# Holding two output chunks of each batch over into the next batch's up phase (landmark attention into a gated product, one core)

## The chip, the core and the metric

The kernel runs on one NeuronCore of a Trainium2 chip. The metric is the device time in microseconds; where several executions are named, it is their median.

## What is computed

There are 8 batches of 8 heads, 576 tokens and head size 64. Queries and keys are averaged over 18 neighbouring tokens into 32 landmarks. Three softmax matrices, an iterated inverse of the 32 x 32 one, and v make the attention; its result, 512 wide, goes through two projections that are multiplied with each other, and two further weights.

```python
A  = sm(q, k_lm);  Bm = sm(q_lm, k_lm);  C = sm(q_lm, k)
Z  = Bm.T / (norm1(Bm) * norminf(Bm) + 1e-06)
for _ in range(6):
    Z = 2 * Z - Z @ Bm @ Z
x = (A @ Z @ C @ v)                 # (batch, tokens, heads*64) -> 4608 x 512
out = (((x @ w1) * (x @ w2)) @ w3) @ w_out      # 4608 x 512, float32
```

## The kernel before, in words

A prologue loads the weights and multiplies `w3 @ w_out` once into `w34` (function `fold`), beside the attention of batch 0. The eight batches then follow. Two things run beside each other in each of them.

The first is the product of batch `b`. `up(st, j, w)` makes one *unit*: four matmuls of 288 columns (line 433) into a PSUM tile `big`. For `w == 0` (called u here) ScalarE copies it to `a_sb` (line 437); for `w == 1` (called v) VectorE multiplies it with `a_sb` into the product tile `ab` (line 439). Sixteen units, j from 0 to 7, fill the 1024 rows of `ab` for the 576 tokens of a batch. `ab` holds two batches, so an even batch has four whole chunks of 128 tokens and an odd one five. `down` makes one *half* of a chunk's output: four matmuls of 512 columns (line 451) into a PSUM bank; after the second half ScalarE scales it into `o_sb` (line 460), and SP's queue writes it out (line 467).

The second is the attention of batch `b + 1`, a generator, advanced one stage at a time by `steps(at)`:

- stage 1: scores of four heads, `big`, exponent on ScalarE (lines 211, 215); the first partial sums on POOL (222 to 227)
- stage 2: the 32 x 32 landmark matrix `psB` (238), its exponent `ebm` (242), then row sums, reciprocal, product and transpose on VectorE (245 to 251)
- stage 3: scores of the other four heads; the norm on VectorE (261 to 268)
- stage 4: `psR` (300) into the one bank of `acc`, read by four VectorE operations (306, 308); `scores_a` (285); two `cv` products with v (317), the first into `small`, the second into `acc`
- stages 5 to 10: the six inverse steps, it0 to it5, each 16 small matmuls into a `big` tile (376), then `tz` and `sz` on VectorE (381, 383), which the next step needs; it0 to it2 add a reciprocal (346), it3 `rhi` and `rmix`, it5 the first `normalise` (361, 364)
- stage 11: `psZ` in `small` (398) and the second `normalise`
- stages 12 and 13: `g`, the weights of the next batch's units (419), moved out by ScalarE and VectorE (423, 425)

The PSUM tiles are three of `big` (two banks each) and one each of `small` and `acc`. The kernel is built under a manual schedule: each engine runs what it is given in the order of the program text, so the calls in the last loop are the order of the work.

For batch `b + 2` three more things are woven in: `turn_all` issues its transposing DMAs on SP (line 106) at the start of the batch; `load_v_piece` puts a small ScalarE copy and a DMA on SP (84, 85); `sums` and `landmarks` run on POOL (176 to 181, 196), with a ScalarE copy `far` in each `landmarks` (195). `sums` also issues the loads of batch `b + 3` from POOL.

In the loop before, the up phase takes stages 1 to 4 of the attention: after units u1, u2, u4 and u6. Stage 5 (it0) follows the last unit. The down phase then takes all chunks of the batch (8 halves in an even batch, 10 in an odd one), with one further stage after each half: it1 to it5, psZ, g, g. The chunks alternate between `acc` and `big`.

Of the kernel before, what the change touches and what calls it, by code (L numbers as in the profile page):

```python
# [13 lines left out]
B = 8  # L14
H = 8
S = 576
# [9 lines left out]
NP = 96  # L26
# [5 lines left out]
def kernel(  # L32
# [20 lines left out]
    def big():  # L53
        return psp.tile([128, 2, 512], FP32, name="big", bufs=3)

    def small():
        return psp.tile([128, 512], FP32, name="small", bufs=1)
# [22 lines left out]
    def load_v_piece(st, b, i, done):  # L80
        if i == 0:
            st["vt"] = pin.tile([128, H, 384], FP32, name="vt")
        hs = slice(2 * i, 2 * i + 2)
        nc.scalar.copy(out=st["vt"][0:NP, 2 * i, 0:1], in_=done)
        nc.sync.dma_start(out=st["vt"][0:NP, hs],
                          in_=v[b, hs].rearrange("h (p r) d -> p h (r d)", p=NP))

    def qk_pieces(st, b):
        st["qkn"] = pin.tile([128, 2, H, 384], FP16, name="qkn")
        for t, src in ((0, q), (1, k)):  # L90
            for i in range(2):
                hs = slice(4 * i, 4 * i + 4)
                nc.gpsimd.dma_start(out=st["qkn"][0:NP, t, hs, :],
                                    in_=src[b, hs].rearrange("h (p r) d -> p h (r d)", p=NP))
                yield
# [29 lines left out]
    ident = consts.tile([128, 128], FP32, name="ident")  # L125
# [45 lines left out]
    def sums(st, t, pieces=iter(())):  # L171
        st["o"] = st.get("o", {})
        o = st["o"][t] = pz.tile([128, H, 32], FP32, name="o%d" % t, bufs=1)
        x = st["qkT"][:, t]
        tr = pat.tile([128, H, NP], FP32, name="tr", bufs=1)
        nc.gpsimd.tensor_tensor(out=tr, in0=x[:, :, 0, :], in1=x[:, :, 1, :], op=ALU.add)  # L176
        nc.gpsimd.tensor_tensor(out=tr, in0=tr, in1=x[:, :, 2, :], op=ALU.add)  # L177
        next(pieces, None)
        t3 = tr.rearrange("p h (l g) -> p h l g", g=3)
        nc.gpsimd.tensor_tensor(out=o, in0=t3[:, :, :, 0], in1=t3[:, :, :, 1], op=ALU.add)  # L180
        nc.gpsimd.tensor_tensor(out=o, in0=o, in1=t3[:, :, :, 2], op=ALU.add)  # L181
        next(pieces, None)

    def landmarks(st, t, parity):
        o = st["o"][t]
        own, other = slice(64 * parity, 64 * parity + 64), slice(64 - 64 * parity, 128 - 64 * parity)
        if parity == 0:
            st["far"] = pz.tile([128, H, 32], FP32, name="far%d" % t, bufs=1)
            if t:
                st["lm"] = pat.tile([128, H, 32], FP16, name="lm")  # L190
            else:
                st["qbd"] = qbds.pop(0)
                qbds.append(st["qbd"])
        far = st["far"]
        nc.scalar.copy(out=far[own], in_=o[other])  # L195
        nc.gpsimd.tensor_tensor(out=st["lm"][own] if t else st["qbd"][own, :, parity, :],  # L196
                                in0=o[own], in1=far[own], op=ALU.add)


    def attention(st, bank=None):  # L200
        bank = bank or small
# [30 lines left out]
        yield  # L232

        lm = st["lm"]
        psB = bank()
        for qd in range(2):
            for h in range(4):
                nc.tensor.matmul(psB[32 * h:32 * h + 32, 32 * qd:32 * qd + 32],
# [129 lines left out]
        for it in range(6):  # L368
# [3 lines left out]
            for h in range(4):  # L372
                for qd in range(2):
                    sl = slice(32 * h, 32 * h + 32)
                    t = h ^ qd
# [34 lines left out]
        g = st["g"] = pat.tile([128, 2, 2, DF], FP16, name="gt")  # L410
# [18 lines left out]
    def up(st, j, w):  # L429
        p = big()  # L430
        for qd in range(2):
            for c in range(2):
                nc.tensor.matmul(p[:, c, 0:HS], st["g"][:, qd, w, 128 * j:128 * j + 128],  # L433
                                 st["ahat"][qd][:, c, :], start=(qd == 0), stop=(qd == 1))
        if w == 0:
            st["a_sb"] = po.tile([128, 2, HS], FP16, name="a_sb", bufs=2)
            nc.scalar.copy(out=st["a_sb"], in_=p[:, :, 0:HS])  # L437
        else:
            nc.vector.tensor_tensor(  # L439
                out=st["ab"][:, j, st["t0"]:st["t0"] + S].rearrange("p (c s) -> p c s", c=2),  # L440
                in0=st["a_sb"], in1=p[:, :, 0:HS], op=ALU.mult)
# [4 lines left out]
    def down(ab, b0, t0, half, hold, bank):  # L446
        if half == 0:
            hold["ps"] = bank()
        pso = hold["ps"]
        for j in range(4 * half, 4 * half + 4):  # L450
            nc.tensor.matmul(pso[:, :], ab[:, j, t0:t0 + 128], w34[:, j, :],  # L451
                             start=(j == 0), stop=(j == 7))
        if half == 1:
            o_sb = po.tile([128, DM], FP32, name="o_sb")
            final = b0 == B - 2 and t0 == 2 * S - 128
            if final:
                nc.vector.tensor_scalar(out=o_sb[:, 256:DM], in0=pso[:, 256:DM],
                                        scalar1=1.0 / (X64 * X64), scalar2=None, op0=ALU.mult)
            c = slice(0, 256 if final else DM)
            nc.scalar.activation(out=o_sb[:, c], in_=pso[:, c], func=AXF.Copy,  # L460
                                 scale=1.0 / (X64 * X64))
            o = 0
            while o < 128:
                gi, p0 = divmod((t0 + o) % S, NP)
                n = min(128 - o, NP - p0)
                eng = nc.scalar if final and o else nc.sync
                eng.dma_start(out=rows[b0 + (t0 + o) // S, 2 * (gi % 3) + gi // 3, p0:p0 + n, :],
                              in_=o_sb[o:o + n, :])
                o += n
# [48 lines left out]
    sts = [dict() for _ in range(B)]  # L518
# [4 lines left out]
    def turn_all(b):  # L523
        for t in (0, 1):
            for h0 in (0, 4):
                transposes(sts[b], t, range(h0, h0 + 4))

    def steps(g, n=1):
        for _ in range(n):
            next(g, None)  # L530
# [3 lines left out]
    with tc.tile_pool(name="pf", bufs=2) as pf:  # L534
# [67 lines left out]
        turn_all(1)  # L602
        steps(fd, 5)
        at = attention(sts[0])
        for n, m in enumerate((2, 2, 3, 3, 2, 1, 1, 1, 1, 2, 2, 3, 3)):
            steps(at)
            if n == 0:
                load_w3(7)
            elif n == 3:
                pieces = qk_pieces(sts[2], 2)  # L610
# [13 lines left out]
        steps(fd, 64)  # L624
    pab = ctx.enter_context(tc.tile_pool(name="pab", bufs=2))
    at = attention(sts[1], acc)


    for b in range(B):
        st = sts[b]  # L630
        if b % 2 == 0:
            ab = pab.tile([128, 8, 2 * S], FP16, name="ab")
        st["ab"], st["t0"] = ab, S * (b % 2)
        if b + 2 < B:
            turn_all(b + 2)
        chunks = range(0, 512, 128) if b % 2 == 0 else range(512, 2 * S, 128)
        for j in range(8):
            up(st, j, 0)
            if b + 1 < B and j == 0:
                landmarks(sts[b + 1], 1, 1)  # L640
            steps(at, (0, 1, 1, 0, 1, 0, 1, 0)[j])
            if b + 2 < B and j > 5:
                load_v_piece(sts[b + 2], b + 2, j - 6, ident[0:NP, 0:1])
            up(st, j, 1)
            if b + 2 < B and j == 5:
                pieces = qk_pieces(sts[b + 3], b + 3) if b + 3 < B else iter(())
                sums(sts[b + 2], 0, pieces=pieces)
                sums(sts[b + 2], 1, pieces=pieces)
        steps(at, 1)
        hold = {}  # L650
        nd = 2 * len(chunks)
        for n in range(nd):
            bank = (lambda: big()[:, 0, :]) if n // 2 % 2 else acc
            down(ab, b - b % 2, chunks[n // 2], n % 2, hold, bank)
            if b + 2 < B and n in (1, 3):
                load_v_piece(sts[b + 2], b + 2, 2 + n // 2, ident[0:NP, 0:1])
            steps(at)
            if b + 2 < B and n in (3, 4, 6):
                landmarks(sts[b + 2], n // 6, (n == 4) + 0)
        steps(at, 30)  # L660
        if b + 2 < B:
            at = attention(sts[b + 2], acc)


# [28 lines left out]
```

## Time and profile before

| what | value |
|---|---|
| median of 7 runs | 281.69 us (279.96 to 286.26) |
| the profiled execution | 280.25 us |
| its span, first to last instruction | 278.5 us |
| TensorE matmul | busy 265.2 us |
| VectorE | busy 164.5 us |
| ScalarE | busy 137.0 us |
| POOL | busy 162.5 us |
| matmuls of the units, line 433 | 512, mean length 286 ns |
| VectorE product, line 439 | 64, mean 749 ns |
| ScalarE copy, line 437 | 64, mean 639 ns |
| matmuls of the output halves, line 451 | 288, mean length 381 ns |

In the profile PE is TensorE's matmuls, PEld its weight loads, DVE VectorE, ACT ScalarE, POOL GpSimd and SP SyncE. The length given for a matmul overlaps with the next one, so distances between starts tell more than lengths. A line of the timeline has start and length in microseconds, engine, source line, tiles written and read, the count of merged instructions, and in brackets the idle time of the engine before it and what ended it.

### The profile page before, as it was taken

The page shows a single profiled execution, that of the slowest core. Times are in us where ns is not written, and L with a number is a line of the kernel's source. Part 1 is how long each engine was busy: PE and PEld are TensorE (multiplying, and loading weights), DVE is VectorE, ACT ScalarE, POOL GpSimd, SP SyncE. Part 2 cuts the span into 40 slices and gives each one's busy share as a digit, 9 for nine tenths or more (in the row PEclk, how much of TensorE's full clock was granted, in tenths as well). Part 3 has the DMA queues.
Part 4 walks back from the last instruction along what each step waited for, and adds up shares of the span by engine and source line. Part 5 has one row for each costly group of instructions (what it writes and reads, how often), then busy time and mean ns, then how long its engine had stood idle before and what let it go on. Part 6 is the DMA issues. An engine that isn't in the chain of part 4 may idle for free.

```text
span 278.5 us, 9481 instructions
## 1 busy us (share of the span) xinstructions
PE 265.2 (95%) x3964; PEld 148.3 (53%) x3964; DVE 164.5 (59%) x439; ACT 137.0 (49%) x259; POOL 162.5 (58%) x210
## 2 busy tenths in 40 slices
PE   7999999999999999999999989999999999999992
PEld 3456555444674476446645744575467346744741
DVE  7744135652476677657765865577668655766710
ACT  2644453144663663466348623762485356615531
POOL 1626862496479759935995699269956944400000
PEclk9999999999999999999999999999999999999998
DMA  6999999999918995999699769895997442014024
GB/s 207 321 239 253 229 271 159 168 277 139 145 44 147 262 170 133 195 213 162 139 209 217 153 133 213 198 162 113 243 225 102 129 153 72 2 47 109 3 75 113
DMA packets 61978, 45.57 MB, mean 164 GB/s; under 512 B 35568, under 2 KB 54000, under 8 KB 61936
## 3 DMA queue, kind: packets, MB, share of 16 engines
q1 hardware_dynamic: 47280, 31.93, 49.6%
q0 software_dynamic: 13824, 11.54, 28.8%
q10 hardware_dynamic: 832, 1.51, 1.5%
q8 instruction: 31, 0.51, 0.8%
q14 instruction: 11, 0.09, 0.1%
HBM read 38.80 MB, written 9.44 MB: 173 GB/s over the span
## 4 chain that ended last, share of the span: by engine, by line
PE 74%; DVE 12%; ACT 8%; issue 3%; DMA 1%; POOL 1%; ACTq 0%; DVEq 0%
PE acc L451 13%; PE big L433 13%; PE acc L497 12%; PE big L451 11%; DVE ab L439 7%; PE big L376 6%; PE big L419 4%; PE small L317 2%; PE big L361 2%; PE small L497 2%; ACT a_sb L437 2%; PE big L484 2%; PE acc L317 2%; ACT gt L423 2%; PE big L211 2%
## 5 line engine op out<-in xcount | busy, mean ns | idle before, releaser
L433 PE MATMUL big<-ahat,gt 128*128 128x288 f16 x512 | 72.8, 286 | 3.3 <-ACT a_sb L437 1.7
L439 DVE TENSOR_TENSOR ab<-a_sb,big 128x576 f16<-128x576 f16 x64 | 47.4, 749 | 24.6 <-ACT a_sb L437 16.1
L433 PEld LDWEIGHTS <-gt 128*128 128x128 f16 x512 | 48.4, 98 | 22.3 <-issue 9.8
L437 ACT CAST a_sb<-big 128x576 f16<-128x576 f32 x64 | 40.9, 639 | 32.2 <-PE big L433 32.1
L497 PE MATMUL acc<-wsp,w3t 128*128 128x512 f16 x168 | 41.1, 380 | 2.0 <-ACT w L500 1.7
L451 PE MATMUL acc<-w,ab 128*128 128x512 f16 x160 | 40.3, 381 | 0.0
L451 PEld LDWEIGHTS <-ab 128*128 128x128 f16 x288 | 24.0, 97 | 29.0 <-issue 4.2
L451 PE MATMUL big<-w,ab 128*128 128x512 f16 x128 | 32.7, 381 | 0.0
L176 POOL TENSOR_TENSOR tr<-qkT 128x768 f32<-128x768 f16 x16 | 26.3, 1641 | 9.0 <-DMA qkT<-qkn 8.8
L460 ACT ACTIVATE o_sb<-acc 128x512 f32<-128x512 f32 (+1 forms) x20 | 11.7, 586 | 37.1 <-PE acc L451 35.5
L497 PEld LDWEIGHTS <-w3t 128*128 128x128 f16 x192 | 17.8, 98 | 21.5 <-issue 3.5
L222 POOL TENSOR_TENSOR t<-ect 96x384 f32<-96x384 f32 x16 | 15.9, 993 | 20.3 <-ACT ect L215 17.3
L425 DVE TENSOR_SCALAR gt<-big 128x1024 f16<-128x1024 f32 x16 | 19.6, 1225 | 13.6 <-PE big L419 13.6
L177 POOL TENSOR_TENSOR tr<-tr,qkT 128x768 f32<-128x768 f32 x16 | 26.3, 1641 | 1.3
L196 POOL TENSOR_TENSOR lm<-o,far 64x256 f16<-64x256 f32 x16 | 11.6, 722 | 26.2 <-ACT far L195 25.7
L423 ACT ACTIVATE gt<-big 128x1024 f16<-128x1024 f32 x16 | 16.4, 1024 | 13.1 <-PE big L419 13.1
L490 DVE SCALAR_TENSOR_TENSOR w3t<-big,w3t 128x512 f16<-128x512 f32 x16 | 11.0, 691 | 19.1 <-ACT w3t L489 19.1
L460 ACT ACTIVATE o_sb<-big 128x512 f32<-128x512 f32 x16 | 9.6, 597 | 16.2 <-PE big L451 16.2
L419 PE MATMUL big<-wup,zt 64*32 64x512 f16 x512 | 17.1, 380 | 0.0
L489 ACT ACTIVATE w3t<-big 128x512 f16<-128x512 f32 x16 | 9.5, 594 | 11.8 <-PE big L484 11.5
L215 ACT ACTIVATE ect<-big 96x768 f32<-96x768 f32 x16 | 12.9, 808 | 2.3 <-PE big L211 2.3
L195 ACT COPY far<-o 64x256 f32<-64x256 f32 x32 | 12.9, 403 | 1.6 <-POOL o L181 0.9
(315 smaller groups left out, 372.5 us busy)
## 6 DMA issues: line engine op xcount, KB each, us to landing
vt<-in_v_dram SPq DMA_DIRECT2D x28, 288.0 KB, 4.2
out_dram<-o_sb SPq DMA_DIRECT2D x23, 192.0 KB, 4.2
qkn<-in_q_dram POOLq DMA_DIRECT2D x12, 288.0 KB, 6.0
qkn<-in_k_dram POOLq DMA_DIRECT2D x12, 288.0 KB, 7.3
w3f<-in_moe_w_dram SPq DMA_DIRECT2D x6, 512.0 KB, 7.6
out_dram<-o_sb SPq DMA_DIRECT2D x24, 128.0 KB, 3.7
wup<-in_moe_w_dram POOLq DMA_DIRECT2D x4, 512.0 KB, 32.0
out_dram<-o_sb SPq DMA_DIRECT2D x24, 64.0 KB, 4.2
```

The source lines that it names most:

```text
L176: nc.gpsimd.tensor_tensor(out=tr, in0=x[:, :, 0, :], in1=x[:, :, 1, :], op=ALU.add)
L177: nc.gpsimd.tensor_tensor(out=tr, in0=tr, in1=x[:, :, 2, :], op=ALU.add)
L376: nc.tensor.matmul(psI[32 * t:32 * t + 32, qd, o:96], tz_[sl, qd, :], sz_[sl, qd, o:96], start=True, stop=True, tile_position=(32 * h, 32 ...
L419: nc.tensor.matmul(psG[32 * h:32 * h + 32, qd, :], zt[rs, i, h, :], wup[rs, h, w, fs], start=(i == 0), stop=(i == 1), tile_position=(64 * ...
L423: nc.scalar.activation(out=g[:, :, w, fs], in_=psG, func=AXF.Copy, scale=1.0 / ZS)
L425: nc.vector.tensor_scalar(out=g[:, :, w, fs], in0=psG, scalar1=1.0 / ZS, scalar2=None, op0=ALU.mult)
L433: nc.tensor.matmul(p[:, c, 0:HS], st["g"][:, qd, w, 128 * j:128 * j + 128], st["ahat"][qd][:, c, :], start=(qd == 0), stop=(qd == 1))
L437: nc.scalar.copy(out=st["a_sb"], in_=p[:, :, 0:HS])
L439: nc.vector.tensor_tensor(out=st["ab"][:, j, st["t0"]:st["t0"] + S].rearrange("p (c s) -> p c s", c=2), in0=st["a_sb"], in1=p[:, :, 0:HS], ...
L451: nc.tensor.matmul(pso[:, :], ab[:, j, t0:t0 + 128], w34[:, j, :], start=(j == 0), stop=(j == 7))
L460: nc.scalar.activation(out=o_sb[:, c], in_=pso[:, c], func=AXF.Copy, scale=1.0 / (X64 * X64))
L497: nc.tensor.matmul(psW[j][:, :], turned[j, c // 4][:, a, c % 4, :], wsp[:, b, c, :], start=(c == 0 and a + b == 0), stop=(c == 7 and a == 1))
```

## The change

The last loop is driven by strings. A token `u3` or `v3` is a unit, `a` one attention stage, `d` one output half, `p` a piece of v, `s` the sums, `h` and `k` landmarks, `g` the landmarks of the batch that comes next; `|` does nothing. Chunks go into a list, `waiting`, when the last unit of their batch has been issued, and each `d` takes the next half from the front of the list.

A batch after its own units does only four (even) or six (odd) halves; four halves, two chunks, stay in the list. In the next batch, `d` tokens among the units take them: two in the first quarter (after v0 and v1), two in the middle (after v4 and u5). Batch 0 (`FIRST`) has nothing to take among its units; batch 7 (`LAST`) takes four halves after v0 to v3 and does ten after its units. A half taken early uses `acc`; of the later ones, chunks alternate as before.

With that the attention stages move. Stage 1 now follows u0, stage 2 u1, stage 3 u2, stage 4 v3; it0 to it3 lie between units 4 and 7, and it4, it5, psZ and both g lie among the remaining halves. `psB` goes to `small` in place of the bank given to `attention`.

```diff
-        psB = bank()
+        psB = small()
...
+    FIRST = "u0 g a v0 u1 a v1 u2 a v2 u3 v3 a s u4 v4 a p u5 v5 a u6 v6 a p u7 v7 a"
+    MIXED = "u0 g a v0 d u1 a v1 d u2 a v2 u3 v3 a s u4 v4 d a p u5 d a v5 u6 a p v6 u7 a v7"
+    EVEN = "a p h d a h d a p d a k d a"
+    ODD = "d a p h d a h d a p d a k d a d"
+    LAST = "u0 v0 d u1 v1 d u2 v2 d u3 v3 d u4 v4 u5 v5 u6 v6 u7 v7" + 10 * " d"
+
+    waiting = []
+
+    def piece(early):
+        item = waiting[0]
+        if item["half"] == 0:
+            item["bank"] = acc if early or item["t0"] // 128 % 2 == 0 else (lambda: big()[:, 0, :])
+        down(item["ab"], item["b0"], item["t0"], item["half"], item, item["bank"])
+        item["half"] += 1
+        if item["half"] == 2:
+            waiting.pop(0)
...
-        for j in range(8):
-            up(st, j, 0)
...
-            steps(at, (0, 1, 1, 0, 1, 0, 1, 0)[j])
...
-            up(st, j, 1)
...
-        steps(at, 1)
-        hold = {}
-        nd = 2 * len(chunks)
-        for n in range(nd):
-            bank = (lambda: big()[:, 0, :]) if n // 2 % 2 else acc
-            down(ab, b - b % 2, chunks[n // 2], n % 2, hold, bank)
...
-            steps(at)
...
+        ups = LAST if b == B - 1 else MIXED if b else FIRST
+        names = (ups + (" | " if b < B - 1 else " ") + (EVEN, ODD)[b % 2] * (b < B - 1)).split()
+        npiece = nhalf = nup = 0
+        for t in names:
+            if t[0] in "uv":
+                up(st, int(t[1]), 0 if t[0] == "u" else 1)
+                nup += 1
+                if nup == 16:
+                    waiting += [dict(ab=ab, b0=b - b % 2, t0=c, half=0)
+                                for c in (range(0, 512, 128) if b % 2 == 0 else range(512, 2 * S, 128))]
+            elif t == "d":
+                piece(nup < 16)
+            elif t == "a":
+                steps(at)
...
```

The other tokens call the same functions as before (`landmarks`, `sums`, `load_v_piece`), at the places that the strings give.

More of the change, by code (lines that the diff above doesn't have):

```diff
@@ L633 @@
         st["ab"], st["t0"] = ab, S * (b % 2)
-        if b + 2 < B:
+        soon = sts[b + 2] if b + 2 < B else None
+        if soon is not None:
             turn_all(b + 2)
-        chunks = range(0, 512, 128) if b % 2 == 0 else range(512, 2 * S, 128)
-        for j in range(8):
-            up(st, j, 0)
-            if b + 1 < B and j == 0:
-                landmarks(sts[b + 1], 1, 1)
-            steps(at, (0, 1, 1, 0, 1, 0, 1, 0)[j])
-            if b + 2 < B and j > 5:
-                load_v_piece(sts[b + 2], b + 2, j - 6, ident[0:NP, 0:1])
-            up(st, j, 1)
-            if b + 2 < B and j == 5:
-                pieces = qk_pieces(sts[b + 3], b + 3) if b + 3 < B else iter(())
-                sums(sts[b + 2], 0, pieces=pieces)
-                sums(sts[b + 2], 1, pieces=pieces)
@@ L649 @@
-        steps(at, 1)
-        hold = {}
-        nd = 2 * len(chunks)
-        for n in range(nd):
-            bank = (lambda: big()[:, 0, :]) if n // 2 % 2 else acc
-            down(ab, b - b % 2, chunks[n // 2], n % 2, hold, bank)
-            if b + 2 < B and n in (1, 3):
-                load_v_piece(sts[b + 2], b + 2, 2 + n // 2, ident[0:NP, 0:1])
-            steps(at)
-            if b + 2 < B and n in (3, 4, 6):
-                landmarks(sts[b + 2], n // 6, (n == 4) + 0)
+        ups = LAST if b == B - 1 else MIXED if b else FIRST
@@ new lines @@
+        names = (ups + (" | " if b < B - 1 else " ") + (EVEN, ODD)[b % 2] * (b < B - 1)).split()
[11 more added lines that the diff above has]
+                steps(at)
+            elif t == "g":
+                landmarks(sts[b + 1], 1, 1)
+            elif soon is not None and t == "s":
+                pieces = qk_pieces(sts[b + 3], b + 3) if b + 3 < B else iter(())
+                sums(soon, 0, pieces=pieces)
+                sums(soon, 1, pieces=pieces)
+            elif soon is not None and t == "p":
+                load_v_piece(soon, b + 2, npiece, ident[0:NP, 0:1])
+                npiece += 1
+            elif soon is not None and t == "h":
+                landmarks(soon, 0, nhalf)
+                nhalf += 1
+            elif soon is not None and t == "k":
+                landmarks(soon, 1, 0)
@@ L660 @@
         steps(at, 30)
-        if b + 2 < B:
-            at = attention(sts[b + 2], acc)
+        if soon is not None:
+            at = attention(soon, acc)
 _INS = ['q', 'k', 'v', 'moe_w1', 'moe_w2', 'moe_w3', 'moe_w_out']
```

## The prediction

> **What bounds the kernel now.** I read the page first (busy shares, then the chain), then the stretch sums by phase, then the timeline of TensorE and VectorE over one batch.
>
> ```profile
> PE 265.2 (95%) x3964; PEld 148.3 (53%) x3964; DVE 164.5 (59%) x439; ACT 137.0 (49%) x259; POOL 162.5 (58%) x210
> PE 74%; DVE 12%; ACT 8%; issue 3%; DMA 1%; POOL 1%; ACTq 0%; DVEq 0%
> ```
>
> TensorE is busy nearly throughout and holds 74% of the chain of waits. Its busy share cannot say how much can still be won, because the modelled ends overlap. So I take starts. This is the up phase of batch 6 in the timeline of TensorE:
>
> ```profile
> 230.45 1.63 PE L433 MATMUL big<-ahat,gt 128*128 128x288 f16 x12
> 231.97 0.70 PE L211 MATMUL big<-qbd,qkT 128*96 128x64 f16 x12
> 232.67 1.14 PE L433 MATMUL big<-ahat,gt 128*128 128x288 f16 x8
> 233.74 0.22 PE L238 MATMUL acc<-lm,qbd 64*32 64x32 f16 x8
> 233.90 1.64 PE L433 MATMUL big<-ahat,gt 128*128 128x288 f16 x12
> 235.78 0.65 PE L433 MATMUL big<-ahat,gt 128*128 128x288 f16 x4 [0.24 <-ACT a_sb L437]
> 236.37 0.68 PE L211 MATMUL big<-qbd,qkT 128*96 128x64 f16 x12
> 237.03 2.38 PE L433 MATMUL big<-ahat,gt 128*128 128x288 f16 x16
> ...
> 241.51 1.65 PE L433 MATMUL big<-ahat,gt 128*128 128x288 f16 x12
> 243.09 0.40 PE L376 MATMUL big<-sz__4579,tz__4580 32*32 32x96 f32 x16
> ```
>
> The columns are start, length, engine, line, tiles, count. Twelve up matmuls in 1.52 us (230.45 to 231.97) give 0.49 us for an up unit of four when nothing is waited for, so the sixteen units need 7.84 us. The attention stages woven between them take 3.78: scores twice 0.63, psB 0.25, and psR with scores_a and both cv 2.27 (about 0.1 at each change of tile shape included). That is 11.62; from 230.45 to the end of the last unit (243.09 less one change) it is 12.54. So TensorE waits 0.92 us in the up phase of an even batch. The same sum for an odd one (203.04 on) gives 1.15. In the down phase, inverse steps follow one another at 1.30 us, which is four matmuls of 512 columns plus one step: no wait there. A whole batch thus has about one microsecond to win out of 26.5 (70.32 to 255.90 is seven batches).
>
> The chain of waits says who makes TensorE wait:
>
> ```profile
> 233.85 0.39 ACT a_sb L437
> ...
> 234.38 0.24 ACT ebm L242
> ...
> 235.60 1.38 DVE ab L439 x2
> ...
> 237.42 0.23 DVE nrn L265
> ...
> 237.96 0.76 DVE ab L439
> ...
> 238.76 0.65 PE big L433 x4
> ```
>
> VectorE works through the softmax and norm of the landmark matrix (rbs to nrn, about 2.0 us of small operations) and must put the up products between them. TensorE then waits for one of the three `big` buffers. It is VectorE's order, not its load (59%), that makes the gap.
>
> **What the skill says.** "TensorE: Matmul & The Clock Gate", section Back-to-back issue gap, gives N/2.4 + 2.5 ns: 122 ns for 288 columns, 216 for 512. The trace agrees (1.52 us for 12; the last down phase has 8 in 1.73), so an output half is 0.86 us. Section "Architectural detail" there says that ScalarE and VectorE are strict FIFO; the trace agrees, as products and softmax pieces run in program order. "Perfetto Trace Analysis", section Identifying the Most-Contended Engine, calls matmul busy share a poor measure of the room left; here 95% stands beside up phases that wait 7 to 9%.
>
> **The change, part by part.** It removes no instruction. Each batch after the first does four output halves between the up units, taken from the batch before; each but the last leaves four over. Sorted by what it moves:
>
> 1. Four inverse steps (it0 to it3) go from the down phase, where halves separate them, to the second half of the up phase, among units 4 to 7. Only two halves lie there in MIXED, and none in FIRST.
> 2. Attention's first four stages come earlier: stage 4 (psR, scores_a, cv) after four unit pairs, not after six and a half.
> 3. psB moves from `acc` to `small`, because `acc` now holds an open half. `small` is free from psZ on: no cost. The early halves use only `acc`, so no `big` buffer is taken from the units.
> 4. Pieces of v, sums and landmarks keep their order on SP, POOL and ScalarE. POOL has slack: it waits 1.9 to 3.6 us per batch for `far`. The copy for the second landmarks sits 2 us or more behind the end of the sums (in batch 0, which shortens most, almost at it). An early output's DMA is queued on SP behind the transposes (about 7 us of issue), but there are three o_sb buffers and only two early outputs a batch, nine microseconds apart: no cost, and if the cover went, one o_sb wait of a microsecond or two a batch.
>
> So the cost lies in the waits. I replay one batch on paper with the trace's durations: a unit is free to be evicted 0.75 after its first matmul; ScalarE's copy takes 0.64 (next start 0.54 later), VectorE's product 0.75 (next 0.69 later); a `big` tile goes to whichever buffer is free first. An inverse step costs TensorE 0.33 and then VectorE these:
>
> ```profile
> 192.31 0.23 DVE L381 TENSOR_TENSOR tz__3634<-big,eye 128x64 f32<-128x64 f32 x1 [0.27 <-PE big L376]
> 192.45 0.35 DVE L383 COPY sz__3636<-big 128x192 f32<-128x192 f32 x1
> 192.71 0.46 DVE L346 RECIPROCAL small<-small 128x48 f32<-128x48 f32 x1
> ```
>
> That step began on TensorE at 191.82: tz starts 0.49 later, sz is ready at 0.98, and VectorE is held 0.81 to 0.86. On the old order the rules give the gaps seen (u4 held to 5.33 after u0, u6 to 8.31), so I trust them to 0.1 or 0.2 us.
>
> *Odd batch, times from u0.* sc0 0.77 (waits for g's buffer), v0 1.41, half 1.90, u1 2.76, psB 3.35, v1 3.50, half 3.99, u2 4.85, sc1 5.44. VectorE: psB's softmax 4.31 to 5.30, v1's product to 6.05, norm to 7.04, v2's and v3's products to 8.70, the four reads of psR to 9.34. So v2 waits until 6.10 (0.13), and the second cv, which needs psR's bank, from 9.03 to 9.37 (0.34). Stage 4 ends at 10.19. Second half: u4, v4, half, it0 at 12.13, u5, half, it1 at 14.15, v5 14.48, u6 14.97, it2 15.56. On VectorE it1 runs 14.64 to 15.45, v5's product to 16.20, it2 to 16.95, v6's product 17.00 to 17.75, it3 17.82 to 18.86, v7's product to 19.61. So v6 waits for v5's buffer from 15.89 to 16.25 (0.36), v7 from 17.66 to 17.80 (0.14), and the units end at 18.29. The work in that stretch is 11.62 + four halves 3.46 + it0 with denominators 0.67 + three steps of 0.43 = 17.04. Waits 1.25 against 1.15: **+0.1** for each of batches 1, 3, 5. From it1 to v7 VectorE has 4.9 us of work beside TensorE's 3.6: that is where the new wait comes from.
>
> *Even batch.* A half lies between g and u0, so the first part is 0.29 shorter and the units end at 18.00 (waits 0.96). But EVEN begins with it4 at once; its copies stand behind v7's product until 19.26, sz is ready at 19.75, and it5 starts 19.85, not 19.41 (0.44). 1.40 against 0.92: **+0.48** for each of batches 2, 4, 6.
>
> *Batch 0 (FIRST).* No halves at all: psB waits for the landmarks 0.41, v2 0.32, scores_a 0.32, cv 0.07, v5 to v7 0.08 + 0.24 + 0.14, and it4 follows it3 with nothing between: sz of it3 behind v7's product gives 1.15. Together 2.7 against 0.9: **+1.8**.
>
> *Batch 7 (LAST).* Before, its 64 matmuls took 8.87 us (255.90 to 264.77) for 7.84 of work. With halves behind the first four pairs only the last four gather waits: **-0.45**.
>
> Sum: 0.3 + 1.44 + 1.8 - 0.45 = +3.1 us. Against the profiled execution (280.25 us, span 278.5, 1.75 around it) that is 283.3. This execution lies 1.44 below the median of the seven runs, and I predict the median: 281.69 + 3.1 = **284.8 us**.
>
> *Not shown by the trace:* a product with another operand in the queue between two inverse steps (taken from the order of the queue: 0.69 each; at least 0, at most 0.75); the buffer choice of the compiler, which fixes by its own estimate which `big` comes free first (taken as right; at worst, by my estimate, one wrong choice per half batch at 0.3, about the distance of two releases in the replay, 4 us in all); denser DMA when batches shorten (the engines' share is 0.75 to 1.03 up to batch 5, yet v lands in 3.6 us and nobody waits; taken at 0, at most 1 us).
>
> **Rivals.** *A, all waits go (faster).* The halves fill every up-phase gap and VectorE keeps pace: 3 x 1.15 + 3 x 0.92 + 0.5 in batch 7, and batch 0 as before: 281.7 - 6.7 = 275.0. For it: the gaps are there, and the early halves stand where they lay. Against it: VectorE's 4.9 us beside 3.6. It decides at v6: if VectorE's work between two inverse steps (0.69 + 0.81 = 1.50) fits TensorE's spacing, 1.41 in MIXED, A holds; half of it would be 278. *B, a wash.* The work on TensorE is the same, and FIRST's loss is milder since POOL and landmarks shift: 281.7. *C, worse.* Two of the four moved steps stand behind a product for its whole length, 2 x 0.69 = 1.4 a batch; less the 0.9 relieved that is 0.5, over seven batches 3.5, and with the wrong buffers' 4 us on top 289. For it: the queue of VectorE is in order. Against it: in the replay the products mostly fall into TensorE's own units.
>
> **How the numbers follow.** Forecast 0.50, A 0.17, B 0.18, C 0.15. The forecast's own range is 282.7 to 287. One per cent, 2.8 us, is about what a measurement here tells from no change. Slower: 0.32 of the forecast and C, 0.47. Same: 0.18 of the forecast, B and a little of A, 0.37. Faster: 0.16. The range reaches half of A and C: 278.5 to 289.
>
> **What would show it.** Right: the up phase has gaps before v6 and v7 with VectorE as releaser; in even batches it5 waits for sz; batch 0 shows a microsecond between it3 and it4; gaps at u4 and u6 of the old order are gone. Wrong: products start within 0.2 us of their unit in the second half of the up phase, or stage 4 runs through without a wait.

## The result and the profile after

The changed kernel takes 283.4 us, the median of 14 runs, against 280.9 for the kernel before in the same measurement. The ratio is 1.0094, with a 95% interval of 1.0071 to 1.0117: slower by 2.6 us, where the prediction summed to +3.1. The ratio, here and below, compares the fast executions alone; some executions of every kernel take longer, at a lower granted clock. The profile below is of a further execution of the same kernel (`after_again`), measured beside the first experiments: 283.10 us, span 281.3 against 278.5 before.

The page of the changed kernel, its busy shares and its chain by engine:

```profile
PE 262.8 (93%) x3964; PEld 149.9 (53%) x3964; DVE 162.5 (58%) x439; ACT 137.9 (49%) x259; POOL 162.7 (58%) x210
PE 79%; ACT 9%; DVE 5%; issue 3%; DMA 1%; POOL 1%; ACTq 0%; DVEq 0%
```

The instruction counts of TensorE, VectorE, ScalarE and POOL are those of before, and so is the work: what can have changed is the waits, and the length of an operation that is held while it runs. VectorE's share of the chain falls from 12% to 5% while the kernel gets slower. A chain names who came last at each step; it is not a sum of waits.

The timeline of TensorE in the second half of an even batch's up phase, from it1 (135.65) on:

```profile
135.65 0.40 PE L376 MATMUL big<-sz__2433,tz__2431 32*32 32x96 f32 x16
135.97 1.15 PE L433 MATMUL big<-ahat,gt 128*128 128x288 f16 x8
137.06 0.40 PE L376 MATMUL big<-sz__2473,tz__2471 32*32 32x96 f32 x16
137.85 1.14 PE L433 MATMUL big<-ahat,gt 128*128 128x288 f16 x8 [0.40 <-ACT a_sb L437]
138.92 0.39 PE L376 MATMUL big<-sz__2500,tz__2498 32*32 32x96 f32 x16
139.42 0.65 PE L433 MATMUL big<-ahat,gt 128*128 128x288 f16 x4
140.06 0.40 PE L376 MATMUL big<-sz__2529,tz__2527 32*32 32x96 f32 x16
140.39 1.04 PE L451 MATMUL acc<-w,ab 128*128 128x512 f16 x4
141.74 0.34 PE L376 MATMUL big<-sz__2552,tz__2550 32*32 32x64 f32 x16 [0.31 <-DVE sz__2552 L383]
```

v5 and u6 start at 135.97, v6 only at 137.85, v7 at 139.42, and it5 at 141.74 though its half had begun at 140.39 and needs 0.86. VectorE in the same stretch:

```profile
136.55 0.46 DVE L346 RECIPROCAL small<-small 128x48 f32<-128x48 f32 x1
136.92 0.74 DVE L439 TENSOR_TENSOR ab<-a_sb,big 128x576 f16<-128x576 f16 x1
137.57 0.21 DVE L381 TENSOR_TENSOR tz__2498<-big,eye 128x64 f32<-128x64 f32 x1
...
140.16 0.36 DVE L352 SCALAR_TENSOR_TENSOR rmix<-rhi,lomask,small 128x144 f16<-128x144 f16 x1
140.44 0.74 DVE L439 TENSOR_TENSOR ab<-a_sb,big 128x576 f16<-128x576 f16 x1
141.11 0.22 DVE L381 TENSOR_TENSOR tz__2550<-big,eye 128x64 f32<-128x64 f32 x1
```

v5's product starts only when it1's reciprocal is nearly over (136.92), v7's when rmix is (140.44), and it4's tz (141.11) when v7's product is. That is the queue that the prediction described.

The table shows u0 to the next batch's u0, from the starts of the up matmuls (batch 7: to its last output matmul). A half takes 0.86 us. Before, in `stages_only` and in `stages_negated` these stretches hold 8, 10, 8 and 10 halves, in the order of the rows; in the changed kernel 4, 10, 8 and 14. The last kernel tried, new_order2, also puts a half ahead of u0 in odd batches, where it counts to the batch before: 5, 9, 9 and 13.

| batch | before | after | stages_only | stages_negated | new_order2 |
|---|---|---|---|---|---|
| 0 | 25.39 | 24.24 | 26.81 | 26.11 | 23.21 |
| odd, undisturbed | 27.41 | 27.56 | 29.02 | 28.32 | 25.50 |
| even (2, 4, 6) | 25.45 | 25.92 | 27.30 | 26.60 | 25.58 |
| 7 | 17.29 | 20.19 | about 16.9 | about 16.9 | 19.05 |

With the four halves put back (3.46 us), batch 0 is 2.31 us slower and batch 7 0.56 faster; odd batches lose 0.15, even ones 0.47. The sum is 2.31 + 0.45 + 1.41 - 0.56 = 3.6. The spans differ by 2.8: 0.26 of the rest lies ahead of batch 0, and the other half microsecond in odd batches that a pause of TensorE disturbs (see the last section). Before, batches 1 and 3 are 0.41 and 1.22 us longer than the undisturbed one, batch 5; in the changed kernel batch 5 is 1.11 longer than batches 1 and 3.

Corrected to the halves of before, new_order2 has 25.80, 26.36, 24.72 and 16.46.

### The profile page after: what moved, and what is told of

Read it like the earlier page. It is cut to its first block, busy times and chain, and to the rows that moved or that the text cites. A ratio compares the mean times of both kernels' runs of the same rounds, so it can differ in the third digit from the quotient of the medians.

```text
span 288.4 us, 9479 instructions
## 1 busy us (share of the span) xinstructions
PE 265.6 (92%) x3964; PEld 150.7 (52%) x3964; DVE 162.6 (56%) x439; ACT 138.0 (48%) x259; POOL 162.6 (56%) x210
## 4 chain that ended last, share of the span: by engine, by line
PE 73%; ACT 8%; DMA 8%; DVE 5%; issue 4%; SPq 0%; ACTq 0%; POOL 0%; DVEq 0%; POOLq 0%
PE big L433 21%; PE acc L451 16%; PE acc L497 9%; DMA w3f<-in_moe_w_dram 8%; PE big L451 5%; PE big L376 4%; PE big L419 4%; DVE ab L439 3%; ACT a_sb L437 2%; PE big L211 2%; PE small L317 2%; ACT gt L423 2%; PE acc L317 2%; PE big L361 2%; PE small L497 2%
## 5 line engine op out<-in xcount | busy, mean ns | idle before, releaser
L433 PE MATMUL big<-ahat,gt 128*128 128x288 f16 x512 | 76.7, 286 | 3.8 <-ACT a_sb L437 2.6
L433 PEld LDWEIGHTS <-gt 128*128 128x128 f16 x512 | 47.0, 98 | 23.9 <-issue 5.5
L451 PE MATMUL acc<-w,ab 128*128 128x512 f16 x216 | 55.1, 380 | 0.0
L497 PE MATMUL acc<-wsp,w3t 128*128 128x512 f16 x168 | 42.8, 391 | 2.3 <-ACT w L500 2.1
L451 PEld LDWEIGHTS <-ab 128*128 128x128 f16 x288 | 26.3, 98 | 26.0 <-issue 4.3
L460 ACT ACTIVATE o_sb<-acc 128x512 f32<-128x512 f32 (+1 forms) x27 | 15.9, 589 | 32.2 <-PE acc L451 27.1
L451 PE MATMUL big<-w,ab 128*128 128x512 f16 x72 | 18.2, 380 | 0.0
L196 POOL TENSOR_TENSOR qbd<-o,far 64x256 f16<-64x256 f32 x16 | 11.6, 726 | 7.1 <-ACT far L195 6.6
```

The lines of the kernel that those rows point to most:

```text
L497: nc.tensor.matmul(psW[j][:, :], turned[j, c // 4][:, a, c % 4, :], wsp[:, b, c, :], start=(c == 0 and a + b == 0), stop=(c == 7 and a == 1))
```

## The experiments

### Moving the stages without holding halves over

```diff
-    MIXED = "u0 g a v0 d u1 a v1 d u2 a v2 u3 v3 a s u4 v4 d a p u5 d a v5 u6 a p v6 u7 a v7"
-    EVEN = "a p h d a h d a p d a k d a"
-    ODD = "d a p h d a h d a p d a k d a d"
+    MIXED = "u0 g a v0 u1 a v1 u2 a v2 u3 v3 a s u4 v4 a p u5 a v5 u6 a p v6 u7 a v7"
+    EVEN = "d a p h d a h d a p d a k d a d d d"
+    ODD = "d a p h d a h d a p d a k d a d d d d d"
```

`LAST` loses its four early halves too.

> The attention stages stand where the change puts them, but no half is held over: each batch does its 8 or 10 halves after its own units. Theory: moving the stages among the units is what costs, and the halves among the units repay most of it. Expected by the replay: psB waits 0.4 for the landmarks, v2 0.3, scores_a 0.2, the second cv 0.4, it1 0.5, v6 0.4, v7 0.15 in each of seven batches; batch 7 without its gain; in all 5.5 us over before and 4 over the changed kernel, about 286.5 us. Rival (the halves are the cost): at most as slow as before, so 3 us below the changed kernel.

The changed kernel, measured beside it:

> The changed kernel as it is, for a profile in the same conditions as the others. Theory (VectorE's order): up phases with waits before v6 (0.4 us) and v7 (0.2), ended by VectorE's product; the second cv of stage 4 waits about 0.4; in even batches it5 waits 0.5 for sz of it4, in batch 0 it4 waits 1.1 for sz of it3. Batches of 27.6 us (odd) and 25.9 (even), the time 0.9% above before. Rival (the halves themselves are the cost, by their place in TensorE's queue and their copies on ScalarE): units wait right behind halves, for a_sb.

`stages_only` took 291.0 us, 1.036 of before (1.026 to 1.046); the changed kernel 1.0095 (1.0063 to 1.0128), with the waits that were expected of it: in an even batch 0.40 us before v6, 0.32 before the second cv and 0.49 before it5. Units behind a half start 0.86 us after it, without a wait. So the direction is that of the theory: the move of the stages costs, and the halves among the units repay most of it. The rival, that the halves are the cost, is out. But the size was missed: 10 us over before, not 5.5. Part of that is the expectation's own sum: the waits that it lists come to 2.35 us a batch, against about 1 before, and so to some 9 us in seven batches. Another part lies before u4, which starts 9.48 us after u0 in batches 1 to 6. VectorE's and POOL's timelines of `stages_only` there:

```profile
105.42 0.22 DVE L265 TENSOR_REDUCE nrn<-csT 128x2 f32<-128x64 f32 x1
105.67 0.70 DVE L266 TENSOR_SCALAR nrn<-nrn 128x2 f32<-128x2 f32 x1
106.41 0.17 DVE L268 RECIPROCAL nrn<-nrn 128x2 f32<-128x2 f32 x1
```

```profile
105.35 0.99 POOL L222 TENSOR_TENSOR t<-ect 96x384 f32<-96x384 f32 x1
```

Line 266 is an operation on two numbers per partition. It takes 0.17 us in all eight attentions of the kernel before, and here 0.70. In seven attentions of seven it begins inside POOL's line 222 and ends 0.03 us after it. "SBUF — State Buffer" of the Trainium skill, section "SBUF: two separate sides", names a port pair that VectorE and GpSimd share under an "exclusive lock": a VectorE operation in a mode that uses two ports, or with two inputs in SBUF against a reading GpSimd, waits for the whole of the other's operation if that one started first. The trace agrees for this operation (float32, SBUF to SBUF, with constants). Its neighbours that reduce, transpose, take a reciprocal or read PSUM keep their lengths whether POOL works beside them or not.

In the changed kernel the same happens once, in batch 0:

```profile
75.63 0.77 DVE L266 TENSOR_SCALAR nrn<-nrn 128x2 f32<-128x2 f32 x1
76.43 0.17 DVE L268 RECIPROCAL nrn<-nrn 128x2 f32<-128x2 f32 x1
76.51 1.42 DVE L439 TENSOR_TENSOR ab<-a_sb,big 128x576 f16<-128x576 f16 x2
```

### The norm without that operation

```diff
-        nc.vector.reduce_max(out=nrn, in_=csT, axis=AX.X)
-        nc.vector.tensor_scalar(out=nrn, in0=nrn, scalar1=-1.0, scalar2=-1e-6,
-                                op0=ALU.mult, op1=ALU.add)
+        nc.vector.reduce_max(out=nrn, in_=csT, axis=AX.X, negate=True)
```

> As stages_only, but the small VectorE operation of line 266 (norm times -1, less 1e-6) is gone: the maximum before it is taken with its sign turned, and the 1e-6 is left out. In stages_only that operation took 0.69 to 0.76 us in seven of eight attentions, where it takes 0.17 in the kernel before, and each time it ended with POOL's operation of line 222. Theory: it was held by POOL's operation; without it stage 4 comes 0.5 us earlier and each of seven batches is 0.5 us shorter: 3.5 us less than stages_only, the up phases as the paper replay had them. Rival: the half microsecond is a wait for POOL's result or for a buffer that only shows there; then another operation takes it over and the time falls by no more than the 0.2 us per batch of the operation itself (1.4 us).

This kernel leaves out the 1e-6. It took 285.5 us, 1.0159 of before (1.0089 to 1.0228). In each of batches 1 to 6 u4 starts 0.70 us sooner (8.78 us after u0, not 9.48), and batches 2, 5 and 6 are 0.70 shorter (1, 3 and 4, which a pause or a delay disturbs in one of the two runs, 1.08, 0.47 and 0.86). No other operation took the wait over:

```profile
102.54 0.22 DVE L265 TENSOR_REDUCE nrn<-csT 128x2 f32<-128x64 f32 x1
102.79 0.17 DVE L266 RECIPROCAL nrn<-nrn 128x2 f32<-128x2 f32 x1
102.88 1.43 DVE L437 TENSOR_TENSOR ab<-a_sb,big 128x576 f16<-128x576 f16 x2
```

The gain is more than the 0.5 to 0.6 of the held time alone, since the operation's own time and its gap go too (0.20 from start to start), and more than the 0.2 of the rival. At 285.5 the kernel is near the 286.5 expected of `stages_only`, though that figure was summed too low. Thus the order of the stages costs 1.6%, and on top of it this operation cost two more.

This also changes the reading of the run before. In the changed kernel line 266 is held in batch 0 alone. Of the 7.4 us between it and `stages_only`, about 3 (0.52 us in each of batches 1 to 6) are not waits that the halves filled: the halves kept the operation apart from POOL's.

### VectorE's queue between it1 and v7

```diff
             if it == 0:
                 denominators()
+                for i in range(3 if st.get("together") else 0):
+                    inverted(i)
             if it < 3:
-                inverted(it)
+                if not st.get("together"):
+                    inverted(it)
```

> The three reciprocals of it0, it1 and it2 all stand at it0, for the attentions of batches 2 to 7 (woven into batches 1 to 6); there VectorE is idle for about 1.1 us before it1's tz. Nothing else moves. Theory: VectorE's queue between it1 and v7 gets 0.8 us shorter, so the wait before v6 falls from 0.4 to 0.15 us and u0-to-u0 by 0.2 in each of six batches: 1.3 us below the changed kernel, 0.4% over before. If ScalarE's copies or the halves were behind the waits, v6 and v7 would start where they did, and the time would stay.

The ratio to before was 1.0046 (1.0014 to 1.0077), where 1.004 was expected. The interval overlaps that of the changed kernel, so the batches have to decide: v6 starts 15.68 us after u0 in an even batch, not 15.99, the batch is 25.61 long, not 25.92, an odd one 27.26, not 27.56, and nothing before it2 moved. The timelines of TensorE and VectorE there:

```profile
141.60 0.40 PE L376 MATMUL big<-sz__2475,tz__2473 32*32 32x96 f32 x16
142.09 1.14 PE L436 MATMUL big<-ahat,gt 128*128 128x288 f16 x8
```

```profile
139.07 1.46 DVE L346 RECIPROCAL small<-small 128x48 f32<-128x48 f32 x3
...
141.29 0.76 DVE L442 TENSOR_TENSOR ab<-a_sb,big 128x576 f16<-128x576 f16 x1
```

The three reciprocals lie where VectorE was idle, and from it2 to v6 TensorE now has 0.49 us between starts, where it was 0.79. One part differs from the prediction: in the changed kernel v6 did not start when v5's product was out (137.66) but when ScalarE had copied u6 (137.80), as the bracket in its line says. The buffer that it was given was u6's, so about 0.14 of that wait is the choice of the buffer. With the reciprocals moved, v6 (142.09) starts before ScalarE's copy of u6 is over (142.35): it got another buffer. The 0.31 us gained can thus hold these 0.14 beside VectorE's share; no run takes the two apart.

### A half between the last inverse steps

Batch 0 keeps six halves, and batch 1 takes two early ones:

```diff
+        if b == 1:
+            ups = ups.replace("v4 d a p u5 d a", "v4 a p u5 a")
-        names = (ups + (" | " if b < B - 1 else " ") + (EVEN, ODD)[b % 2] * (b < B - 1)).split()
+        names = (ups + (" | " if b < B - 1 else " ") + (EVEN, ODD)[b % 2 or b == 0] * (b < B - 1)).split()
```

> Batch 0 does six of its eight halves itself (in the order of an odd batch, a half between it3 and it4) and holds over one chunk; batch 1 takes that one after v0 and v1 only. Everything else as in the changed kernel. Theory: the wait of it4 for sz of it3, 1.1 us in batch 0, goes, as a half lies between; batch 1 is about 0.1 us worse or 0.2 better without its second pair. In all 0.7 us less than the changed kernel, 0.6 to 0.7% over before. Rival (batch 0 is slow for its units without halves): the same time.

The time was 284.4 us, 1.0126 of before (1.0039 to 1.0213), and so undecided against the changed kernel. In its profile the prologue has a pause of 1.30 us and batch 1 one of 0.71. Batches 1 and 2 also lose 0.26 each at v2, to another VectorE operation that POOL holds, line 248, which has two inputs in SBUF. VectorE and POOL in batch 2:

```profile
127.39 0.48 DVE L248 TENSOR_TENSOR bm<-ebm,rbs 128x64 f32<-128x64 f32 x1
```

```profile
127.34 0.45 POOL L227 TENSOR_TENSOR es<-es,t 96x128 f32<-96x128 f32 x1
```

In the changed kernel line 248 takes 0.23 us. Batch 0 itself answers the question. With two more halves (1.73 us) it grew by 0.85 only, from 24.24 to 25.09: 0.88 us of waiting went. In the changed kernel the two steps stood like this:

```profile
85.48 0.39 PE L376 MATMUL big<-sz__1382,tz__1380 32*32 32x96 f32 x16
86.96 0.40 PE L376 MATMUL big<-sz__1411,tz__1409 32*32 32x96 f32 x16 [1.08 <-DVE sz__1411 L383]
```

A step needs 0.33 us of TensorE, so 1.15 of the 1.48 between the starts is a wait, as predicted; some of it came back as the later steps took over VectorE's delay.

Even batches 2, 4 and 6 keep six halves, and 3, 5 and 7 take two early ones:

```diff
+    MIXED2 = "u0 g a v0 u1 a v1 u2 a v2 u3 v3 a s u4 v4 d a p u5 d a v5 u6 a p v6 u7 a v7"
+    LAST2 = "u0 v0 d u1 v1 d u2 v2 u3 v3 u4 v4 u5 v5 u6 v6 u7 v7" + 10 * " d"
...
+        if b % 2 and b > 1:
+            ups = LAST2 if b == B - 1 else MIXED2
+        names = (ups + (" | " if b < B - 1 else " ") + (EVEN, ODD)[b > 0] * (b < B - 1)).split()
```

> Batches 2, 4 and 6 do six halves themselves (the order of an odd batch) and hold over one chunk; batches 3, 5 and 7 take it, in 3 and 5 after v4 and u5. Theory: it5's wait for sz of it4 in even batches (0.5 us) goes, against some 0.4 us more in batches 3 and 5, which lose the halves after v0 and v1; 0.9 us less than the changed kernel. Rival (each half among the units is worth the same wherever it lies): the loss of two early halves in 3, 5 and 7 outweighs it, no gain.

1.0101 of before (1.0009 to 1.0193): no gain. Even batches did what was expected (27.18 us; 25.92 and two halves would be 27.65, so 0.47 of waiting went). Batches 3 and 5 lost 1.04 instead of 0.4 (26.87 against 27.56 less 1.73). Their u4 stands at 9.48, as in `stages_only`: without the halves after v0 and v1 the norm falls on POOL's line 222 again. The halves in the first quarter thus also kept the two apart. Nobody had planned that.

### Both edits to VectorE's work in the changed order

> The changed kernel with its own order, and two edits to VectorE's work: the reciprocals of it0 to it2 together at it0 (attentions of batches 2 to 7), and the norm's sign turned in its maximum, without the 1e-6. Theory: 0.3 us less in each of batches 1 to 6 from the reciprocals, 0.7 less in batch 0, where line 266 took 0.77 us, and 0.1 to 0.2 in the others from a shorter norm: 3 to 3.5 us less than the changed kernel, level with before. If VectorE's queue is not what the change runs into, it stays near 0.5% over before, as with the reciprocals alone.

1.0046 (1.0015 to 1.0077), where about 1.0 had been expected. That is the figure of the reciprocals alone, and so the rival's: the whole time does not speak for the theory, the batches do in part. Batch 0 gave the 0.7 us (23.53), five of batches 1 to 6 the 0.3 of the reciprocals; the 0.1 to 0.2 for a shorter norm did not come: u4 stands at 10.18 and 9.80 as before. The sum, 2.2 us over the batches, was in the profiled span too (279.3 against 281.3).

### Another order of the same tokens

```diff
+    FIRST = "u0 g v0 u1 a v1 a a u2 v2 u3 a v3 s u4 a v4 a p u5 v5 u6 a v6 a p u7 v7"
+    MIXED = ("u0 g v0 a u1 d v1 a u2 a d v2 u3 a v3 s u4 a v4 p u5 v5 u6 a p d a v6 u7 a d v7",
+             "u0 d g v0 u1 a v1 a a u2 d v2 u3 a v3 s u4 a v4 p a d u5 v5 u6 a d a p v6 u7 v7 d")
+    EVEN = "p a h d a h d a d p a k d a"
+    ODD = "p a d a d a d h a h d a p k d"
+    ZERO = "d p a h d a a h d p a k d a"
+    LAST = "u0 d v0 u1 v1 d u2 v2 u3 d v3 u4 v4 u5 v5 d u6 v6 u7 v7" + 10 * " d"
```

The pair under MIXED is for even and odd batches; ZERO is what batch 0 does after its units.

> Only the order of the strings is new: psB stands after the first or second unit pair, the norm follows two tokens later, so that VectorE's chain of psB and norm is over before stage 4; each inverse step has a half or two units between it and the next, and behind each product a step is not waited for at once. Four halves are still held over (batches 0 to 6). Theory: TensorE's work is unchanged, so what goes is waits alone, and the replay leaves 0.1 to 0.4 us of them in a batch: odd batches 26.3 us, even ones 24.8, batch 0 22.5, and about 9 us less than the changed kernel, 274 us. Rival (holding halves over costs by itself): no faster than before.

0.9961 (0.9910 to 1.0011): not below before with certainty, and far from 274. Line 266 took 0.67 us in even batches and about 0.25 in odd ones; in the trace scores_a waits 0.72 us in even batches and 0.30 in batch 1, for VectorE's product. So the same order was run with the sign turned:

> As new_order, with the norm's sign turned in its maximum (line 266's operation and the 1e-6 left out). In new_order that operation took 0.67 us instead of 0.17 in the attentions woven into batches 2, 4 and 6, where POOL's operation of line 222 runs beside it, and 0.25 in four others. Theory (it is held by POOL): even batches 0.5 to 0.7 us shorter, odd ones 0.1 to 0.3, 2 to 3 us in all; about 1.2% below before. Rival (the replay misses something else in stage 4, such as the choice of the big buffer): scores_a keeps its wait of 0.4 (odd) and 0.8 us (even) and the time stays at 0.4% below before.

0.9898 (0.9843 to 0.9953). Even batches fell from 25.38 to 24.70, by 0.68, as the theory said. Batch 1 stayed at 27.00, but not because nothing was gained: its v3, behind stage 4, starts 0.25 us sooner (8.97 us after u0, not 9.22), within the 0.1 to 0.3 expected, and a pause behind it, 0.43 us long here and 0.17 in new_order, takes that back.

A last order was sought with the mended figures:

```diff
+    FIRST = "u0 g v0 u1 a v1 a u2 v2 u3 a v3 s u4 a v4 p u5 a v5 u6 a v6 a p u7 v7 d a"
+    MIXED = ("u0 g v0 u1 d a v1 a u2 d a v2 u3 a v3 s u4 a v4 p u5 a d v5 u6 a d p a v6 u7 v7",
+             "d u0 g v0 u1 a v1 a u2 d a v2 u3 a v3 s u4 v4 d p a u5 a v5 u6 p a d a v6 u7 v7")
+    EVEN = "d a p d h a d h a d a p a k"
+    ODD = "d a d p a d a h h p d k a d a d"
+    ZERO = "d p a d a a h h d a p a k"
+    LAST = "d u0 v0 u1 v1 u2 d v2 u3 v3 d u4 v4 u5 v5 d u6 v6 u7 v7" + 10 * " d"
```

> Another order, found with the replay after its figures for the norm were mended (no operation of line 266, the exponent of psB 0.1 later), and the same turned sign. Four halves are held over; psB, the norm and stage 4 stand one unit pair apart from each other, halves stand between inverse steps in the middle of the up phase and two before the last ones. Theory: waits of 0.1 to 0.3 us in a batch are left, odd batches 25.4 to 26.8 us, even ones 25.2 to 26, about 6 us (2%) below before, 275 us. Rival (holding halves over costs by itself, in whatever order): not below before.

274.9 us, 0.9757 of before (0.9707 to 0.9807), and so faster than both kernels, by 2.4 and about 3%. Batches 1 and 3 take 25.60 and 25.50 us, even ones 25.58; with 10 and 8 halves, as before, they would take 26.36 (batch 3) and 24.72, where it was 27.41 and 25.45. Batch 5 of the profiled execution (278.23 us) takes 28.90:

```profile
207.60 0.24 PE L320 MATMUL acc<-ones,es 96*32 96x1 f32 x7 [1.71 <-issue]
207.78 1.90 PE L431 MATMUL big<-ahat,gt 128*128 128x288 f16 x12
209.47 1.91 PE L449 MATMUL acc<-w,ab 128*128 128x512 f16 x4
```

A pause of 1.71 us is followed by 3.41 us in which the granted clock is 0.5, and a half takes 1.84 us from start to start. The stretch sums of batches 1 and 2 of this kernel (length; then busy time of TensorE, weight loads, VectorE, ScalarE and POOL; clock, DMA share, GB/s):

```profile
95.40:121.00 25.60, 25.51 (x457) 14.75 (x456) 17.39 (x46) 14.32 (x28) 20.78 (x26) 1.00 1.09 188
121.00:146.58 25.58, 25.23 (x458) 14.96 (x457) 17.58 (x46) 14.89 (x29) 19.37 (x24) 1.00 1.05 192
```

and those of an odd and an even batch of the changed kernel:

```profile
147.78:175.35 27.57, 26.56 (x469) 15.34 (x462) 18.09 (x47) 15.19 (x29) 20.07 (x25) 1.00 0.92 188
121.86:147.78 25.92, 24.80 (x453) 14.71 (x452) 16.54 (x46) 14.07 (x29) 20.13 (x25) 1.00 0.91 169
```

Each has about one microsecond of the stretch in which no matmul ran in the changed kernel (27.57 less 26.56), and 0.1 to 0.35 here. The halves held over are the same four per batch. Denser transfers (shares of 1.09 and 1.05) cost nothing in these two batches that a wait would show. The rival that holding halves over costs by itself, in whatever order, is out. What the norm's edit would give the kernel before was not run: there line 266 takes its 0.17 us and is never held, so that at 0.20 from start to start it could be worth at most 1.4 us in seven batches, of the 6.2 between the medians.

## Why the prediction was right

- *The mechanism and the sum.* Predicted +3.1 us, measured +2.6. TensorE's work was unchanged and the difference was waits, mostly in VectorE's queue order. The forecast time, 284.8, lies 1.4 above the 283.4 found; 0.8 of that is its starting point, a median of seven executions (281.69) that 35 put at 280.9. That the sum comes so close is in part luck: in the two profiles the batches lose 3.6 us, and pauses and the prologue, which the prediction did not treat, take 0.8 of it back.
- *The spacing of matmuls.* The prediction used N/2.4 + 2.5 ns. The section of the Trainium skill that it names, "Back-to-back issue gap" in "TensorE: Matmul & The Clock Gate", gives that for a single matmul, and about 131 ns at 512 columns for a stream with weight loads. Here each matmul has its weight load, and eight of 512 columns take 1.73 us to the start of the next, 216 ns each: the formula fits, the lower figure does not.
- *Odd batches, +0.1 each.* Measured +0.15. The times from u0 came out at u1 2.74 (2.76), v1 3.48 (3.50), v2 5.95 (6.10), u4 10.18 (10.19), v5 14.48 (14.48), v6 16.36 (16.25), v7 17.93 (17.80).
- *Even batches, +0.48 each.* Measured +0.47, with it5 waiting for sz behind v7's product.
- *Batch 7, -0.45.* Measured -0.56.
- *Batch 0, +1.8.* Measured +2.31: the one term that was clearly mis-sized. The 1.15 between it3 and it4 came out to the hundredth, which is luck in a replay trusted to 0.1 or 0.2; the missing half microsecond is stage 4, where scores_a and the second cv waited about 0.9 instead of 0.39, behind line 266's 0.77 us; without that operation (the run with both edits) batch 0 is 0.71 us shorter. Nothing in the trace of before showed that operation beside POOL's line 222, and the prediction let VectorE's durations stand unchanged when their neighbours changed.
- *v6's releaser* was to be VectorE; it was ScalarE's copy of u6, through the choice of the buffer. The prediction carried that choice only in its range. Of the 0.36 us by which v6 is late, 0.22 is the queue and 0.14 the buffer.
- *Rival A* (all waits go, 275) fails for this order: at v6 VectorE's queue made most of the wait. But the time it named is to be had with the same held-over halves in another order and without line 266. *B* is outside the interval. *C* charged the choice of buffers with 4 us in all; what the trace shows of it is 0.14 at v6. The move of psB to `small`, put at no cost, is in every run of the new loop and was not tried alone.

## What to carry to other kernels

When work is moved that had been another chain's cover, replay both chains: the halves did fill the gaps among the units, but the inverse steps they had covered were moved into a place where a queue in order put products between them. A count of the gaps gives the most that can be won; who is queued behind whom gives the sign. And when two engines are moved against each other in time, look once for operations whose length has changed, not only for waits.

## What the runs showed of the hardware that was not expected

A VectorE operation on 128 x 2 float32 numbers in SBUF took 0.67 to 0.77 us instead of 0.17 whenever it began inside one POOL operation of 1.0 us, and then ended with it; begun in the last tenths of a shorter one it took 0.25. Taking it away was worth 0.70 us per batch. An operation with two inputs in SBUF (line 248) took up to 0.48 instead of 0.23 in the same way, and where both began within 0.01 us it was POOL's that took 0.53 instead of 0.45.

TensorE also pauses, mostly in the middle of a row of small matmuls, with no wait that the profile names. In the changed kernel:

```profile
210.60 0.86 PE L317 MATMUL acc<-vt,ect 96*32 96x64 f32 x45 [0.31 <-PE small L322]
212.29 0.25 PE L317 MATMUL acc<-vt,ect 96*32 96x64 f32 x2 [0.82 <-issue]
```

The place follows from the count of instructions, not from the work. Pauses of this kind longer than 0.15 us stand in the batches of eleven of the twelve profiles, seventeen in all (0.17 to 1.76 us). Each comes after 2,753, 4,545 or 6,337 of TensorE's records, weight loads included, or after one more; these places are 1,792 apart. The page lists transfers of instructions among its DMA queues:

```profile
q8 instruction: 31, 0.51, 0.7%
```

Each of the 31 moves 16,384 bytes, and each of the seventeen pauses ends 1.29 to 1.56 us after the 10th, the 17th or the 24th of them has landed. So the traces point to TensorE waiting for its own instructions. No run changed how they are loaded, so this is read off the traces and not tried. A change in the order of the work moves the pauses to another stage and can make them longer: batch 5 loses 0.82 us in the changed kernel and 1.71 in new_order2. There the granted clock fell to 0.5 behind the pause. That is why single batches without a pause were compared first and whole times second.
